# Gate/up groups in fours with shared remainders, one PSUM tag, and x transposed by DMA, in a fused state-space and gated-unit kernel

## The chip, the core and the metric

One core of one Trainium2 chip. The metric is the device time of one execution in microseconds (us), the median of several. The profile's span runs from the first to the last instruction and is about 1.8 us shorter than the time. TensorE is PE below, its weight loads PEld, VectorE DVE, ScalarE ACT, SyncE SP; SPq and ACTq are their instruction streams issuing DMAs. PSUM is the memory in which matmuls add up their results; a slot is the piece of it that a group of matmuls holds until ACT has copied it out (its drain).

## The reference, cut to what matters

```python
xn = layernorm(x)                               # x: 1 x 2048 x 576, bf16
# A: diagonal complex state space, 576 states
Bu = einsum("bld,pd->blp", xn, B_bar)
h[t] = Lam_bar * h[t-1] + Bu[t]                 # 2048 steps
yA = 2 * real(einsum("blp,dp->bld", h, C)) + xn * Dskip
# B: gated unit, F = 4608
yB = (sigmoid(xn @ w_gate) * (xn @ w_up)) @ w_down
out = x + yA + yB
```

## The kernel before

The 2048 rows are four blocks (`nb`) of 512, handled two at a time; F is cut in three, so there are six stages of 24 gate/up groups and 8 down-projection steps. Contraction 576 is four times 128 and a remainder of 64 rows: the remainder matmuls of gate (upper 64 rows of the array) and up (lower 64) run side by side. A scheduler (`bg`) strews the LayerNorm of later blocks and the state-space work on DVE between the groups. A normalised tile is `xn`, its transpose `xT`; `brre` holds the remainder rows of B, `hst` the states, `acc` the running sum of a row tile. Cut:

```python
def ln_transpose(tt):                           # one of 16 row tiles
    ptr = psum.tile([P, NXK, P], BF16, name="ptr", tag="pg")
    for k in range(NXK):
        nc.tensor.transpose(ptr[:, k, :], xn[:, c0:c0 + P], ident[:])
    nc.scalar.copy(xT[nb][:, :, tl * P:(tl + 1) * P], ptr[:])
# ...
def gu_step(sb, c, f, nb):                      # one gate/up group
    pg = psum.tile([P, TB], FP32, name="pg", tag="pg")
    pu = psum.tile([P, TB], FP32, name="pu", tag="pu")
    rem_first = (nb % 2 == 0)
    if rem_first: rem()                         # two 64-row matmuls
    for (ps, gi) in ((pg, 0), (pu, 1)):
        for k in range(KF):
            nc.tensor.matmul(ps[:], w[:, gi, k, fs], xt_[:, k, :], ...)
    if not rem_first: rem()
    nc.scalar.activation(sT[:], pg[:], ACT.Sigmoid)
    nc.scalar.copy(uT[:], pu[:])
    nc.vector.tensor_mul(h[:], sT[:], uT[:])
# ... start: blocks 0 and 1 are normalised and transposed whole, with
# their residuals, before the first group; later: queue_ln per tile:
#     ln_stats, ln_rstd (square root on ACT), ln_norm, ln_transpose, ln_resid
# ... second stage: load_ct (four C transposes by DMA), then
def pack_bt():
    nc.sync.dma_start(brre[0:H, :], brre[H:P, :])
```

Of the kernel before, what the change touches and what calls it, by code (L numbers as in the profile page):

```python
# [19 lines left out]
ROW_TILED = True  # L20


class Background:



    def __init__(self):
        self.queue = deque()
        self.credit = 0.0

    def add(self, cost, fn):
        self.queue.append((cost, fn))

    def step(self, us):
        self.credit = min(self.credit + us, 4.0)
        while self.queue and self.queue[0][0] <= self.credit:
            cost, fn = self.queue.popleft()
            self.credit -= cost
            fn()

    def drain(self):
        while self.queue:
            self.queue.popleft()[1]()
# [3 lines left out]
def kernel(  # L47
# [19 lines left out]
    H = 64  # L67
# [7 lines left out]
    TB = 512  # L75
    NB_SB = 2
    NSB = S // (TB * NB_SB)
# [3 lines left out]
    PT = NS // P  # L81
    FC = 12
    NC = F // P // FC
    DH = D // 2
    XW = R0 + 2 * H if ROW_TILED else R0 + 3 * H
    NXK = KF + 1 if ROW_TILED else KF + 2
    T_G = 1.95 if ROW_TILED else 2.16
# [9 lines left out]
    evp = ctx.enter_context(tc.tile_pool(name="evp", bufs=3))  # L97
    ssmp = ctx.enter_context(tc.tile_pool(name="ssmp", bufs=1))
    psum = ctx.enter_context(tc.tile_pool(name="psum", bufs=2, space=bass.MemoryType.PSUM))


    def load_x(tt, eng):
        xt = lnp.tile([P, D], BF16, name="xt", bufs=6)
        eng.dma_start(xt[:], x[tt * P:(tt + 1) * P, :])
        return xt
# [4 lines left out]
    def load_wgu(key, pair, eng):  # L110
        f0 = pair * 2 * P
        w = wpool.tile([P, 2, KF, 2 * P], BF16, name="wgu", bufs=3)
        wr = wpool.tile([P, 2 * P], BF16, name="wrem", bufs=3)
        fs = slice(f0, f0 + 2 * P)
        eng.dma_start(w[:, 0], B_w_gate[0:R0, fs].rearrange("(k p) f -> p k f", p=P))
        eng.dma_start(wr[0:H, :], B_w_gate[R0:D, fs])
        eng.dma_start(w[:, 1], B_w_up[0:R0, fs].rearrange("(k p) f -> p k f", p=P))
        eng.dma_start(wr[H:P, :], B_w_up[R0:D, fs])
        wgu_t[key] = (w, wr)
# [7 lines left out]
    xts = {}  # L127
    for tt in range(TT_B):
        xts[tt] = load_x(tt, nc.sync)
    load_wgu((0, 0), 0, nc.scalar)  # L130

    ident = consts.tile([P, P], BF16, name="ident")
    make_identity(nc, ident[:])
# [4 lines left out]
    XN_BUFS = 3  # L138
    xn_bufs = []
    for i in range(XN_BUFS):  # L140
        xn_i = consts.tile([P, XW], BF16, name=f"xn{i}")
        if not ROW_TILED:
            nc.vector.memset(xn_i[:, D:D + H], 0.0)
        xn_bufs.append(xn_i)

    for tt in range(TT_B, 2 * TT_B):
        if tt < 6:
            xts[tt] = load_x(tt, nc.sync)
    load_wgu((0, 1), 1, nc.sync)
    dskip_rows = consts.tile([P, D], BF16, name="dskip_rows")  # L150
    nc.gpsimd.dma_start(dskip_rows[:], A_Dskip.partition_broadcast(P))


    BN = nc.vector.BN_STATS_DIM
    mvs = {}
    accs = {}
# [3 lines left out]
    def ln_stats(tt):  # L160
        xt = xts[tt]
        st = lnp.tile([P, 2, BN], FP32, name="bnst", bufs=2)
        for gi in range(2):
            nc.vector.bn_stats(st[:, gi, :], xt[:, gi * DH:(gi + 1) * DH])  # L164
        mv = lnp.tile([P, nc.vector.BN_AGGR_DIM], FP32, name="mv", bufs=10)
        nc.vector.bn_aggr(mv[:], st[:])
        mvs[tt] = mv

    rstds = {}

    def ln_rstd(tt):
        r = lnp.tile([P, 1], FP32, name="rstd", bufs=10)
        nc.scalar.activation(r[:], mvs[tt][:, 1:2], ACT.Sqrt, bias=eps_t[:], scale=1.0)
        rstds[tt] = r

    xns = {}

    def ln_norm(tt):
        xn = xn_bufs[ln_count[0] % XN_BUFS]
        ln_count[0] += 1  # L180
        r = rstds[tt]
        nc.vector.reciprocal(r[:], r[:])
        nc.vector.tensor_scalar(xn[:, 0:D], xts[tt][:], mvs[tt][:, 0:1], r[:], ALU.subtract, ALU.mult)  # L183
        nc.vector.tensor_copy(xn[:, XW - H:XW], xn[:, R0:D])
        xns[tt] = xn

    def ln_transpose(tt):
        nb, tl = divmod(tt, TT_B)
        if tl == 0:
            xT[nb] = hpool.tile([P, NXK, TB], BF16, name="xT", bufs=3)  # L190
        xn = xns[tt]
        ptr = psum.tile([P, NXK, P], BF16, name="ptr", tag="pg")
        for k in range(NXK):
            c0 = k * P if k <= KF else R0 + H
            nc.tensor.transpose(ptr[:, k, :], xn[:, c0:c0 + P], ident[:])  # L195
        nc.scalar.copy(xT[nb][:, :, tl * P:(tl + 1) * P], ptr[:])  # L196

    def ln_resid(tt):
        tmp = lnp.tile([P, D], BF16, name="tmpxd", bufs=1)
        nc.vector.tensor_mul(tmp[:], xns[tt][:, 0:D], dskip_rows[:])  # L200
        acc = accp.tile([P, D], FP32, name="acc", bufs=16)
        nc.vector.tensor_add(acc[:], xts[tt][:], tmp[:])  # L202
        accs[tt] = acc


    for tt in range(TT_B):
        ln_stats(tt)
        ln_rstd(tt)
        if tt >= 1:
            ln_norm(tt - 1)  # L210
            ln_transpose(tt - 1)
        if tt >= 2:
            ln_resid(tt - 2)
    ln_norm(TT_B - 1)
    ln_transpose(TT_B - 1)
    ln_resid(TT_B - 2)
    ln_resid(TT_B - 1)
    for tt in range(6, 2 * TT_B):
        xts[tt] = load_x(tt, nc.sync)
    for tt in range(TT_B, 2 * TT_B):  # L220
        ln_stats(tt)
        ln_rstd(tt)
        ln_norm(tt)
        ln_transpose(tt)
        ln_resid(tt)
    for pr in range(2, 3):
        load_wgu((0, pr), pr, nc.sync)
    load_wd((0, 0), 0, nc.sync)


    NU = PT + 1
# [9 lines left out]

    def load_bt():
        W0 = D - P
        nc.sync.dma_start_transpose(btre[:], A_B_re[:, 0:R0])
        nc.sync.dma_start_transpose(brre[:], A_B_re[:, W0:D])
        nc.sync.dma_start_transpose(btim[:], A_B_im[:, 0:R0])
        nc.sync.dma_start_transpose(brim[:], A_B_im[:, W0:D])

    def load_ct():
        W0 = NS - P  # L250
        nc.sync.dma_start_transpose(ctre[:], A_C_re[:, 0:R0])
        nc.sync.dma_start_transpose(ctim[:], A_C_im[:, 0:R0])
        nc.sync.dma_start_transpose(ctp[:], A_C_im[:, W0:NS])
        nc.sync.dma_start_transpose(ctw[:], A_C_re[:, W0:NS])
        nc.sync.dma_start(ctp[0:H, :], ctw[H:P, :])

    def pack_bt():
        if ROW_TILED:
            nc.sync.dma_start(brre[0:H, :], brre[H:P, :])
# [4 lines left out]
        if not ROW_TILED:  # L264
            nc.gpsimd.memset(btp[0:H, KF, :], 0.0)


    lre = consts.tile([P, NU], FP32, name="lre")
    lim = consts.tile([P, NU], FP32, name="lim")
    ldt = consts.tile([P, NU], FP32, name="ldt")  # L270
    for (dst, src) in ((lre, A_Lambda_re), (lim, A_Lambda_im), (ldt, A_log_dt)):
        for pt in range(PT):
            nc.gpsimd.dma_start(dst[:, pt:pt + 1], src[pt * P:(pt + 1) * P].rearrange("(a b) -> a b", b=1))
        for h0 in (0, H):
            nc.gpsimd.dma_start(dst[h0:h0 + H, PT:NU], src[R0:NS].rearrange("(a b) -> a b", b=1))
    sg_pm = consts.tile([P, 1], FP32, name="sg_pm")
    nc.gpsimd.memset(sg_pm[0:H, :], 1.0)
    nc.gpsimd.memset(sg_pm[H:P, :], -1.0)
    iota = consts.tile([P, TB], FP32, name="iota")
    nc.gpsimd.iota(iota[:], pattern=[[1, TB]], base=0, channel_multiplier=0,  # L280
                   allow_small_or_imprecise_dtypes=True)

    r5 = consts.tile([P, NU], FP32, name="r5")
    thc = consts.tile([P, NU], FP32, name="thc")
    qre = consts.tile([P, NU], FP32, name="qre")
    qim = consts.tile([P, NU], FP32, name="qim")
    nqre = consts.tile([P, NU], FP32, name="nqre")
    c512 = consts.tile([P, NU], FP32, name="c512")
    s512 = consts.tile([P, NU], FP32, name="s512")
# [8 lines left out]
    def sincos(u, sin_out, cos_out):  # L298
        a = small("sc_a")
        b = small("sc_b")  # L300
        for (dst, add) in ((sin_out, 0.0), (cos_out, 0.25)):
            nc.vector.tensor_scalar_add(a[:], u[:], add)
            nc.vector.tensor_scalar_add(b[:], a[:], MAGIC)
            nc.vector.scalar_tensor_tensor(b[:], b[:], MAGIC, a[:], ALU.subtract, ALU.subtract)
            nc.scalar.activation(dst[:], b[:], ACT.Sin, bias=zero_t[:], scale=SIN_SCALE)

    def per_state():
        dt = small("dt")
        nc.scalar.activation(dt[:], ldt[:], ACT.Exp)
        nc.vector.tensor_mul(r5[:], dt[:], lre[:])  # L310
        nc.scalar.activation(r5[:], r5[:], ACT.Exp)
        nc.vector.tensor_mul(thc[:], dt[:], lim[:])
        nc.vector.tensor_scalar_mul(thc[:], thc[:], 1.0 / TWO_PI)
        sn, cs = small("sn"), small("cs")
        sincos(thc, sn, cs)
        u = small("u512")
# [364 lines left out]
```

## Time and profile before

| | before |
|---|---|
| time, median | 620.75 us |
| span | 618.7 us |
| PE busy | 543.7 us (88%) |
| granted PE clock, mean | 0.956 |
| PE waiting for the norms (DVE) | 50.9 us |
| PE waiting for the remainder rows of B (`brre`) | 10.2 us |

Read it from PE: an idle microsecond there is on the chain that ends last, and an idle microsecond of DVE or ACT is not. In a wait row the columns are: who waited, `<-` for whom, us in total, times, longest.

### The profile page before, as it was taken

The numbers are of one execution on the slowest core, as the hardware profiler recorded it, in microseconds if no ns is written. First come the engines' busy times: TensorE is split into PE (matmuls) and PEld (weight loads), VectorE is DVE, ScalarE is ACT, GpSimd is POOL, SyncE is SP. The second block draws the span as 40 slices with busy tenths as digits, with TensorE's granted clock in tenths as the row PEclk, the third lists the DMA queues.
The fourth block names the chain that finished last, engine by engine and source line by source line (L and its number), as shares of the span: only waits on it lengthen the run. The fifth ranks groups of instructions, "written<-read, shape, count | busy, mean of one in ns | idle before, by whom it ended". The sixth has DMA issues, their size and how long they took to land.

```text
span 618.7 us, 8129 instructions
## 1 busy us (share of the span) xinstructions
PE 543.7 (88%) x3140; PEld 282.2 (46%) x3140; DVE 327.8 (53%) x738; ACT 229.8 (37%) x395; POOL 13.0 (2%) x34
## 2 busy tenths in 40 slices
PE   1399979957999997666889999999999999999967
PEld 1133357422357432223664333763335763336745
DVE  6711259772576573322244665674656665555451
ACT  3355543533530465551014555115553025552000
POOL 7000000000000000000000000000000000000000
PEclk9999999997999997777899999999999999999979
DMA  7227520262230142113000423202423012400000
GB/s 164 56 58 173 153 58 0 59 146 72 69 108 1 39 122 66 56 45 101 18 17 2 114 80 95 58 0 59 116 77 95 1 40 63 145 4 11 30 11 29
DMA packets 72405, 40.34 MB, mean 65 GB/s; under 512 B 17424, under 2 KB 72336, under 8 KB 72368
## 3 DMA queue, kind: packets, MB, share of 16 engines
q1 hardware_dynamic: 68896, 39.09, 22.8%
q0 software_dynamic: 2256, 0.16, 0.6%
q10 hardware_dynamic: 1216, 0.59, 0.3%
q8 instruction: 24, 0.39, 0.3%
q14 instruction: 13, 0.11, 0.1%
HBM read 34.36 MB, written 2.36 MB: 59 GB/s over the span
## 4 chain that ended last, share of the span: by engine, by line
PE 80%; DVE 11%; ACT 4%; DMA 2%; SPq 2%; issue 1%; ACTq 0%; DVEq 0%
PE pd L546 26%; PE pg L524 21%; PE pu L524 20%; PE pg L518 6%; PE pa L385 2%; PE pb L385 2%; DVE bnst L164 1%; DVE xn L183 1%; PE ptr L195 1%; PE pa L389 1%; DVE acc L202 1%; ACT L535 1%; ACT uT L536 1%; DVE rnd L346 1%; DVE acc L567 1%
## 5 line engine op out<-in xcount | busy, mean ns | idle before, releaser
L524 PEld LDWEIGHTS <-wgu 128*128 128x128 bf16 x1152 | 109.0, 100 | 157.1 <-issue 45.7
L538 DVE TENSOR_TENSOR hT<-sT,uT 128x512 bf16<-128x512 bf16 x144 | 60.5, 422 | 186.8 <-ACT uT L536 186.7
L546 PE MATMUL pd<-wd,hT 128*128 128x288 bf16 x1152 | 151.5, 294 | 4.8 <-DVE acc L567 4.8
L524 PE MATMUL pg<-xT,wgu 128*128 128x512 bf16 x576 | 155.6, 394 | 0.0
L524 PE MATMUL pu<-xT,wgu 128*128 128x512 bf16 x576 | 152.7, 389 | 0.0
L535 ACT ACTIVATE sT<-pg 128x512 bf16<-128x512 f32 x144 | 86.0, 597 | 127.3 <-PE pu L519 101.1
L546 PEld LDWEIGHTS <-hT 128*128 128x128 bf16 x1152 | 114.6, 100 | 39.3 <-issue 8.0
L536 ACT CAST uT<-pu 128x512 bf16<-128x512 f32 x144 | 83.9, 582 | 24.2 <-PE pu L524 24.2
L195 PE MATMUL ptr<-ident,xn 128*128 128x128 bf16 x80 | 10.6, 292 | 50.9 <-DVE xn L183 50.9
L519 PE MATMUL pu<-xT,wrem 64*128 64x512 bf16 x144 | 47.4, 393 | 0.0
L518 PE MATMUL pg<-xT,wrem 64*128 64x512 bf16 x144 | 47.4, 393 | 0.0
L567 DVE TENSOR_TENSOR acc<-acc,pd 128x576 f32<-128x576 f32 x36 | 26.9, 751 | 26.5 <-PE pd L546 26.5
L564 DVE TENSOR_TENSOR ob<-acc,pd 128x576 bf16<-128x576 f32 x16 | 12.0, 753 | 53.8 <-PE pd L546 53.8
L546 PEld LDWEIGHTS <-hst 128*128 128x128 bf16 x288 | 27.9, 98 | 13.5 <-DVE hst L467 5.3
L393 ACT COPY bure<-pa 128x512 f32<-128x512 f32 x16 | 9.4, 585 | 62.9 <-PE pb L390 62.9
L195 PEld LDWEIGHTS <-xn 128*128 128x128 bf16 x80 | 6.8, 127 | 55.5 <-DVE xn L183 55.5
L546 PE MATMUL pd<-ctim,hst 128*128 128x288 bf16 x128 | 26.2, 286 | 0.7 <-DVE hst L473 0.7
L546 PE MATMUL pd<-ctre,hst 128*128 128x288 bf16 x128 | 26.2, 286 | 0.3 <-DVE hst L467 0.3
L437 DVE TENSOR_TENSOR_SCAN gre<-r,g0re,wre 128x512 bf16<-128x512 f32 x20 | 25.5, 1277 | 0.0
L518 PEld LDWEIGHTS <-wrem 64*128 64x128 bf16 x144 | 9.1, 94 | 32.7 <-issue 32.6
L405 ACT COPY bure<-pa 128x512 f32<-128x512 f32 x4 | 2.3, 585 | 52.9 <-PE pa L400 36.3
L196 ACT COPY xT<-ptr 128x640 bf16<-128x640 bf16 x16 | 11.1, 692 | 25.9 <-PE ptr L195 25.9
(118 smaller groups left out, 375.2 us busy)
## 6 DMA issues: line engine op xcount, KB each, us to landing
wd<-in_B_w_down_dram SPq DMA_DIRECT2D x36, 288.0 KB, 3.6
wgu<-in_B_w_gate_dram SPq DMA_DIRECT2D x35, 256.0 KB, 2.9
wgu<-in_B_w_up_dram SPq DMA_DIRECT2D x35, 256.0 KB, 3.6
xt<-in_A_x_dram SPq DMA_DIRECT2D x16, 144.0 KB, 3.4
out_dram<-ob SPq DMA_DIRECT2D x16, 144.0 KB, 1.8
wrem<-in_B_w_gate_dram SPq DMA_DIRECT2D x35, 32.0 KB, 2.6
wrem<-in_B_w_up_dram SPq DMA_DIRECT2D x35, 32.0 KB, 3.2
wgu<-in_B_w_gate_dram ACTq DMA_DIRECT2D x1, 256.0 KB, 3.4
```

Of the source, the lines that this page charges most:

```text
L195: nc.tensor.transpose(ptr[:, k, :], xn[:, c0:c0 + P], ident[:])
L385: nc.tensor.matmul(ps[:], bt[:, k, cols], xt_[:, k, :], start=(k == 0), stop=False)
L437: nc.vector.tensor_tensor_scan(gre[:], r_bc, tmps["wre"][:], g0re[:, col], ALU.mult, ALU.add)
L518: nc.tensor.matmul(pg[:], wr[0:H, fs], xt_[0:H, KF, :], start=rem_first, stop=not rem_first)
L519: nc.tensor.matmul(pu[:], wr[H:P, fs], xt_[H:P, KF, :], start=rem_first, stop=not rem_first)
L524: nc.tensor.matmul(ps[:], w[:, gi, k, fs], xt_[:, k, :], start=(k == 0 and not rem_first), stop=(k == KF - 1 and rem_first))
L535: nc.scalar.activation(sT[:], pg[:], ACT.Sigmoid)
L536: nc.scalar.copy(uT[:], pu[:])
L538: nc.vector.tensor_mul(h[:], sT[:], uT[:])
L546: nc.tensor.matmul(pd[:, a, 0:DH], lhsT, rhs[:, a * DH:(a + 1) * DH], start=first, stop=last)
L564: nc.vector.tensor_add(halves(ob[:]), halves(acc[:]), pd[:, :, 0:DH])
L567: nc.vector.tensor_add(halves(acc[:]), halves(acc[:]), pd[:, :, 0:DH])
```

## The change

Intent: keep PE's stream free of waits and of switches between 64-row and 128-row matmuls. Core of the diff; the rest is scheduling and renaming.

```diff
-    psum = ... bufs=2                      # tags pg, pu and pd
+    psum = ... bufs=PE_SLOTS               # 4 slots of two banks, one tag "ps"
+    def emit_cluster(groups):              # four gate/up or state-input groups
+        first, second = groups[:n1], groups[n1:]
+        for g in first:  g.open(); g.full(True, False)
+        for g in second: g.open()
+        for g in first:  g.rem(False, True)
+        for g in second: g.rem(True, False)
+        for g in first:  g.evac()
+        for g in second: g.full(False, True); g.evac()
-    ln_transpose (PE) for every tile
+    def ln_dma_transpose(tt):              # blocks 1, 2 and 3
+        nc.sync.dma_start_transpose(xT_tile(nb)[:, :, tl*P:(tl+1)*P], xns[tt][:])
+    # block 0: PE transposes, and the first two groups take it tile by tile
+    # as 128-column matmuls, after 8 matmuls on a zero tile
+    for tt in range(TT_B + 1):
+        if tt < TT_B: ln_stats(tt); ln_std(0, tt, tt + 1)
+        if tt >= 1: ln_recip(...); ln_norm(tt - 1); start_transpose(tt - 1)
+        if tt >= 2: start_mms(tt - 2)
+    exp_first()                            # the state space's exponentials
+    # then in the background: residuals 0, 1; loads of x tiles 6, 7;
+    # statistics of block 1; one square root for four tiles; norms, transposes
+    bt_loads = [...]                       # B transposes and pack_bt, one a cluster, stage 1
     load_wgu: bufs=3 -> 4;  wd: one pair beyond those done, as before, but two pairs now end together
+    last output step in two halves, each added and sent by itself
```

## The prediction

> **What bounds the kernel now.** I read the page first (its head and slices), then the waits of TensorE alone, then TensorE's timeline around the longest waits, and last the timelines of VectorE at the start and of the Sync queue.
>
> ```profile
> span 618.7 us, 8129 instructions
> PE 543.7 (88%) x3140; PEld 282.2 (46%) x3140; DVE 327.8 (53%) x738; ACT 229.8 (37%) x395; POOL 13.0 (2%) x34
> ...
> PE   1399979957999997666889999999999999999967
> ...
> PEclk9999999997999997777899999999999999999979
> ```
>
> PE is the longest engine and the chain that ended last is 80% PE. The dips (the first slice, slice 9, slices 16 to 19, the last) are where it waits, and the clock falls in most of the same slices. Idle PE is 618.7 - 543.7 = 75.0 us. The waits name nearly all of it:
>
> ```profile
> engine line waited for: us in total, times, longest us
> PE ptr L195 <- DVE xn L183: 50.9, 16, 7.0
> PE pa L389 <- DMA brre<-brre: 10.2, 1, 10.2
> PE pd L546 <- DVE acc L567: 4.8, 3, 3.5
> PE pd L546 <- DVE hst L467: 4.7, 2, 4.4
> ```
>
> 50.9 + 10.2 + 4.8 + 5.4 (with a 0.7 us row for another hst line) = 71.3, and PE's tail after its last matmul is 3.6: 74.9. Of the 50.9, 23.4 lie in the first 29 us, 27.5 in the middle, where blocks 2 and 3 are normalised between matmuls. One such place:
>
> ```profile
> 233.31 1.03 PE L524 MATMUL pu<-xT,wgu 128*128 128x512 bf16 x4
> 234.27 0.39 PE L518 MATMUL pg<-xT,wrem 64*128 64x512 bf16 x1
> 234.27 0.39 PE L519 MATMUL pu<-xT,wrem 64*128 64x512 bf16 x1
> 238.49 0.72 PE L195 MATMUL ptr<-ident,xn 128*128 128x128 bf16 x5 [3.83 <-DVE xn L183]
> 239.14 0.60 PE L518 MATMUL pg<-xT,wrem 64*128 64x512 bf16 x1
> 239.14 0.61 PE L519 MATMUL pu<-xT,wrem 64*128 64x512 bf16 x1
> 239.68 1.89 PE L524 MATMUL pg<-xT,wgu 128*128 128x512 bf16 x4
> ```
>
> The transpose stands in PE's in-order stream and waits 3.83 us. Afterwards four matmuls take 1.89 us instead of 1.03. In starts, the pitch of a 512-column matmul is 427 ns instead of 216. Counting such matmuls after every gap gives some 20 us of slow running on top of the 75: 2.0 at the start, 2.7 after the brre wait, 1.7 in the first down-projection, 11.3 in the middle, 2.7 near the end. The third cost is in steady state:
>
> ```profile
> 208.40 0.39 PE L518 MATMUL pg<-xT,wrem 64*128 64x512 bf16 x1
> 208.40 0.39 PE L519 MATMUL pu<-xT,wrem 64*128 64x512 bf16 x1
> 208.62 0.38 PE L518 MATMUL pg<-xT,wrem 64*128 64x512 bf16 x1
> 208.63 0.38 PE L519 MATMUL pu<-xT,wrem 64*128 64x512 bf16 x1
> 208.94 0.82 PE L524 MATMUL pg<-xT,wgu 128*128 128x512 bf16 x3
> ```
>
> Remainder pairs run side by side and follow each other at 0.22 us, but the step from 64 to 128 rows takes 308 ns instead of 217, and the step into it 312 instead of 216: 0.187 us for both. I count 198 such steps, 99 pairs, 18.5 us.
>
> **What the Trainium skill says.** "TensorE: Matmul & The Clock Gate", Part 1: the array runs at half clock until it was busy for about 3.4 us and falls back after an idle window as long; the 427 and 216 ns agree, and so do the slow stretches after gaps of 3.8 to 5.5 us. "TensorEngine Tiling (Array Packing)", Key Properties: changing the tiling mode drains the array; the 0.187 us agrees. "ScalarE: Activation LUTs", What ACT_TABLE_LOAD costs: about 1283 ns for every switch of set; the trace has 1283 ns each time, and normalisation (square root) between sigmoids pays it twice. "DMA: Bandwidth & Descriptors", DMA Transpose (X-bar): transposes go out from Sync or ScalarE only and stand beside ordinary DMAs; here 128-column transposes of A_B hold the Sync queue 1.25 us each and land after 3.1 to 4.4.
>
> **The change part by part.**
> 1. Steady work. 1296 matmuls of 512 columns x 0.2163 = 280.3; 164 remainder pairs or singles x 0.220 = 36.1; 1440 of 288 columns x 0.1226 = 176.5; 80 transposes 8.8; 18.5 of row switches: 520.2. After: the same matmuls. A cluster of four groups pays one pair of switches: 164 groups (144 gate/up, 20 state-input) with part clusters and single catch-ups make about 49 clusters, 9.2 us: 9.3 saved. One PSUM tag of four two-bank slots is the whole PSUM; in steady state a slot is reopened 4 us or more after its group's stop, and one group's drain is 0.60 + 0.58 on ACT, so PE should not wait; ACT needs 4.7 us in a cluster of 8.
> 2. Start. Before, the first gate/up matmul is at 29.06 and two groups are done at about 34.9. After, only block 0's four tiles are on this path, without the residual (0.45 + 0.76 us a tile). VectorE per tile is 1.03 + 0.16 + 0.43 + 0.18 = 1.8 us from about 6.3 (DMA 3.0, square-root table 1.28, as before), so the last norm ends near 11.7. PE per tile is 5 transposes (0.6) plus 16 matmuls of 128 columns, 0.107 each cold: 2.3 us, so PE is the later one: 7.2 to about 16, remainders near 17. Saved 34.9 - 17 = 17.9, cold part included.
> 3. Middle. Blocks 2 and 3 leave PE's stream: 27.5 + 11.3 cold = 38.8, and 8 transposes of 0.53 = 4.2 (block 1's are in part 2).
> 4. brre. B transposes are issued one per cluster and packed in the first stage, long before use; C's come later: 10.2 + 2.7 = 12.9.
> 5. Angles move under the gate/up groups, and PSUM for the down-projection is four deep: 4.8 + 1.7 = 6.5.
> 6. The state chain: VectorE per unit 9.4 us, 20 units 166; my sum of the budget that the new scheduler hands out per stage ends the chain in the fifth stage, so the last stage doesn't wait: 5.4 + 2.7 = 8.1. The split last output saves 0.4.
> Removed: 9.3 + 17.9 + 38.8 + 4.2 + 12.9 + 6.5 + 8.1 + 0.4 = 98.1.
> 7. Added: block 1 comes due after only eight groups of block 0, at 17 + 12.5 = 29.5. Its chain: VectorE is blocked by the first exponential (behind ACT's copy of tile 3 and a table load) until about 16.5; two residuals 2.4, two statistics 2.1, two products 0.9, two more statistics 2.1: 24; ACT's square root between two table loads, then the third group's sigmoid and copy and product: 27.3; reciprocal and four norms of 0.6: 30; four transposes at some 1.3 us each on the Sync queue, the last one landing 3 later: 33 to 35. PE waits about 5 and then runs cold for a while: 7.5 in all. The late sigmoid also delays a PSUM slot, inside the same wait.
> 8. Added, small: down-projection weights are now fetched one pair ahead instead of two, state-input groups as clusters of one in down-projection stages: 3.
> Net 98.1 - 10.5 = 87.6: 620.7 - 87.6 = 533. From the other side: PE resumes on block 1 at 34.5, 498 us of steady work less eight groups (12.5) remain, 2 cold, 3 small, 3.2 tail: 530.7 span, and the times stand about 2 above the span: 532.6. I take 532.
>
> **The rivals.**
> A. Block 1 is ready in time, or its wait is 2 us: 524 to 527. For it: the transposes may overlap in the queue, and warm matmuls at the start may leave the clock up. Against it: VectorE's in-order queue as counted in 7.
> B. VectorE becomes the bound. Its 328 us would be 62% of 530, and in stages 2 and 3 products (0.42) plus background (1.37) fill 1.8 of each 2.0 us. If the scheduler's costs are below the real ones (an angle is booked 1.35, its three instructions here take 0.48 + 0.43 + 0.69 = 1.6), VectorE falls behind, output buffers of ACT fill, PE waits: 545 to 560. For most pieces the booked costs are at or above the trace's (1.85 against 1.79), so I give it little.
> C. The Sync queue. Transposes, weight fetches and loads that wait for VectorE share one in-order queue; a weight pair held back behind a transposition wait costs PE 2 to 4 us and a cold restart, once a stage: 540 to 550. Four buffers instead of three speak against it.
> D. All waits were hidden anyway: excluded, since PE's idle time here is on the chain that ends last.
>
> **Range and chances.** The sure part (parts 1, 3, 4) is 65 us. The start and block 1 are uncertain by 5 either way, B and C by 10 upward, A by 7 downward: 521 to 546. Faster by over 2% is anything under 608; all the additions would have to be eight times as large to lose it: 0.98.
>
> **What would show it.** Step 1: about half as many 64/128 switches, still 308 to 312 ns. Step 2: first full-width gate/up group near 17 us. Steps 3 and 4: no PE wait on xn after the first 20 us and none on brre; clock at full in the middle slices. Steps 5 and 6: no PE wait on acc or hst over 1 us. Step 7: a PE wait near 30 us whose releaser is the DMA of xT. Step 8: none over 1 us at the stage borders. It would be wrong if PE shows new waits on ACT's drains (PSUM slots) or on weight DMAs, or if the pitch in clusters is not 216 ns.

## The result, and the profile after

The changed kernel takes 526.53 us (525.29 to 526.59, 4 runs), before 620.75 (620.28 to 621.76, 4 runs). The ratio is 0.8476, 95% interval 0.8459 to 0.8492. A ratio here and below is the mean time of one kernel's fast runs over that of the other's of the same rounds, so not quite the ratio of the medians.

The page's head, and its slices of PE and of the granted clock:

```profile
span 524.7 us, 7898 instructions
PE 508.6 (97%) x3096; PEld 283.5 (54%) x3136; DVE 319.3 (61%) x716; ACT 200.2 (38%) x367; POOL 9.3 (2%) x25
...
PE   7879999999999999999999999999999999999997
...
PEclk9989999999999999999999999999999999999999
```

Only the first three slices and the last one have holes. PE's waits:

```profile
PE pgu L463 <- DMA xT<-xn: 3.8, 1, 3.8
PE pgu L463 <- ACT uT L475: 1.6, 1, 1.6
...
PE pd L557 <- DVE ob L565: 0.5, 1, 0.5
```

No wait is left on `brre`, `acc` or `hst`; on xn 1.5 us, at the start. The first two rows are both of the start: the wait for block 1, and a PSUM slot held by a late drain. PE's timeline there (start, duration, instruction, count, and in brackets the idle time before it and its releaser), and the Sync queue's line for the four transposes:

```profile
27.83 1.67 PE L463 MATMUL pgu<-xT,wgu 128*128 128x512 bf16 x7 [0.16 <-issue]
33.26 5.08 PE L463 MATMUL pgu<-xT,wgu 128*128 128x512 bf16 x15 [3.75 <-DMA xT<-xn]
```

```profile
26.45 5.29 SPq L232 DMA_TRANSPOSE xT<-xn  x4
```

PE finishes block 0's eight groups at 29.5 and waits until block 1 has been normalised and four transposes of 1.3 us each have gone out one behind the other. Then fifteen matmuls take 5.08 us, where fifteen take 3.40 elsewhere: eight starts in a row stand some 427 ns apart, as after the wait in the prediction.

In steady state a cluster looks like this (a state-input group, `pbu`, and three gate/up groups):

```profile
101.93 0.39 PE L503 MATMUL pbu<-xT,brre 64*128 64x512 bf16 x1
101.93 0.39 PE L503 MATMUL pbu<-xT,brim 64*128 64x512 bf16 x1
102.15 0.81 PE L468 MATMUL pgu<-xT,wrem 64*128 64x512 bf16 x6
102.90 3.63 PE L463 MATMUL pgu<-xT,wgu 128*128 128x512 bf16 x16
```

All four groups' remainders follow one another and there is one return to 128 rows. The traces have 198 changes between 64 and 128 rows before and 96 after. The first down-projection, before and after:

```profile
79.85 6.05 PE L546 MATMUL pd<-wd,hT 128*128 128x288 bf16 x48
89.39 7.71 PE L546 MATMUL pd<-wd,hT 128*128 128x288 bf16 x48 [3.48 <-DVE acc L567]
```

```profile
66.88 23.68 PE L557 MATMUL pd<-wd,hT 128*128 128x288 bf16 x192
```

Before, it ran from 79.85 to 110.40 with three waits for `acc`; after, all 192 matmuls stand in one piece. (Some PE records are missing from the traces, so PE's busy time after is a little too low; the gaps above are not of that kind.)

### The profile page after: what moved, and what is told of

Same layout as the page of the kernel before. It is cut to its first block, busy times and chain, and to the rows that moved or that the text cites. A ratio compares the mean times of both kernels' runs of the same rounds, so it can differ in the third digit from the quotient of the medians.

```text
span 524.7 us, 7898 instructions
## 1 busy us (share of the span) xinstructions
PE 508.6 (97%) x3096; PEld 283.5 (54%) x3136; DVE 319.3 (61%) x716; ACT 200.2 (38%) x367; POOL 9.3 (2%) x25
## 4 chain that ended last, share of the span: by engine, by line
PE 94%; DVE 3%; DMA 1%; issue 1%; ACT 1%; ACTq 0%
PE pgu L463 46%; PE pd L557 34%; PE pgu L468 6%; PE pbu L498 6%; PE pbu L503 1%; DVE bnst L206 1%; DMA xt<-in_A_x_dram 1%; DMA xT<-xn 1%; DVE acc L238 0%; PE ptr L718 0%; DVE xn L220 0%; DVE hT L477 0%; DVE tmpxd L236 0%; ACT L474 0%; ACT L299 0%
## 5 line engine op out<-in xcount | busy, mean ns | idle before, releaser
L463 PE MATMUL pgu<-xT,wgu 128*128 128x512 bf16 (+1 forms) x1170 | 259.6, 375 | 7.8 <-DMA xT<-xn 3.8
L474 ACT ACTIVATE sT<-pgu 128x512 bf16<-128x512 f32 x144 | 86.9, 604 | 142.3 <-PE pgu L468 106.1
L475 ACT CAST uT<-pgu 128x512 bf16<-128x512 f32 x144 | 84.7, 588 | 0.0
L576 DVE TENSOR_TENSOR acc<-acc,pd 128x576 f32<-128x576 f32 x32 | 24.1, 752 | 30.3 <-PE pd L557 30.3
L468 PE MATMUL pgu<-xT,wrem 64*128 64x512 bf16 x288 | 38.7, 378 | 0.0
L407 DVE TENSOR_TENSOR_SCAN gre<-r,g0re,wrim 128x512 bf16<-128x512 f32 x20 | 25.6, 1278 | 0.0
L414 DVE TENSOR_TENSOR_SCAN gim<-r,g0im,wrim 128x512 bf16<-128x512 f32 x16 | 20.4, 1274 | 0.0
L498 PE MATMUL pbu<-xT,btim 128*128 128x512 bf16 x62 | 16.3, 379 | 0.1
L498 PE MATMUL pbu<-xT,btre 128*128 128x512 bf16 x57 | 16.1, 379 | 0.4
L393 DVE TENSOR_TENSOR wrim<-T,bure 128x512 bf16<-128x512 bf16 x20 | 13.7, 685 | 0.0
L394 DVE TENSOR_TENSOR tq<-T,buim 128x512 bf16<-128x512 bf16 x20 | 13.7, 685 | 0.0
```

What stands on the lines that cost most here:

```text
L393: nc.vector.tensor_mul(w, t1, a[:])
L407: nc.vector.tensor_tensor_scan(gre[:], r_bc, w[:, 0, :], g0re[:, col], ALU.mult, ALU.add)
L414: nc.vector.tensor_tensor_scan(gim[:], r_bc, w[:, 1, :], g0im[:, col], ALU.mult, ALU.add)
L463: nc.tensor.matmul(self.ps[:, gi, cols], self.w[:, gi, k, self.fs], xT[self.nb][:, k, cols], start=start and k == 0, stop=stop and k == KF ...
L468: nc.tensor.matmul(self.ps[:, gi, :], self.wr[rows, self.fs], xT[self.nb][rows, KF, :], start=start, stop=stop)
L474: nc.scalar.activation(sT[:], self.ps[:, 0, :], ACT.Sigmoid)
```

## Experiments

Twelve runs, eleven variants and the changed kernel again, all with the right result, in three batches of four, each on one chip. "Before" was 621.2, 621.8 and 621.5 us in the three batches, and the changed kernel run again in the third batch took 526.54.

**1. Before, with blocks 2 and 3 transposed by DMA alone.**

```diff
     def ln_transpose(tt):
+        if nb >= 2:
+            nc.sync.dma_start_transpose(xT[nb][:, :, tl*P:(tl+1)*P], xn[:])
+            return
```

> The kernel before with one part of the change alone: the tiles of blocks 2 and 3 are transposed by DMA instead of by TensorE. My theory (TensorE pays for waiting in its own stream, plus slow matmuls afterwards): 27.5 us of waits, 11.3 us of slow matmuls and 4.2 us of transposes go, so about 578 us (573 to 588), and the middle slices show the full clock. Rival (the wait only moves: the normalisation chain on VectorE is what is late, and the next reader of the transposed block waits instead): 600 us or more, with a new TensorE wait on the transposed block.

Measured 579.52 us (ratio 0.9328, 0.9299 to 0.9356), 41.7 us less. The stretch from 233 to 292 us, before and in this run; the columns are the stretch, its length, busy us with instruction counts of PE, PEld, DVE, ACT and POOL, clock, DMA share and GB/s:

```profile
233.00:292.00 59.00, 40.20 (x171) 16.45 (x168) 17.16 (x46) 27.91 (x40) 0.00 (x0) 0.77 0.21 58
```

```profile
233.00:292.00 59.00, 57.00 (x379) 35.19 (x382) 32.38 (x85) 26.23 (x41) 0.00 (x0) 1.00 0.40 96
```

In these 59 us PE is busy 57.00 us instead of 40.20 and the clock is 1.00 instead of 0.77. (The counts are no measure of the work: 264 of the 379 are the shorter 288-column matmuls, before 42 of the 171.) PE's wait for the norms falls to 23.9 us, which is the start, and its wait for the DMA's xT is 0.2 us; new are 1.4 us of waits on ACT. The rival, that the wait only moves to the next reader, falls.

**2. Before, with the copy of B's remainder rows right behind B's transposes.**

```diff
     def load_bt():
         ...
+        nc.sync.dma_start(brre[0:H, :], brre[H:P, :])
     def pack_bt():
-        nc.sync.dma_start(brre[0:H, :], brre[H:P, :])
```

> The kernel before with one line moved: the copy of the B remainder rows goes out right behind the B transposes in the first stage instead of behind the C transposes in the second. My theory: the 10.2 us wait and about 2.7 us of slow matmuls go: 608 us (606 to 611). Rival (the state-input group would then wait for something else that is late as well, or the Sync queue holds back weights in the first stage): 614 us or more, with a new wait of TensorE.

Measured 607.07 us (ratio 0.9775, 0.9748 to 0.9802): 14.1 us less, clear of noise, and no row for `brre` among PE's waits. In the chain that ended last, before, the copy stands behind C's transposes, and PE had been waiting since 132.9:

```profile
129.84 3.16 SPq L251
...
137.38 3.04 DMA ctw<-in_A_C_re_dram
141.05 2.04 DMA brre<-brre
```

One transfer queued behind unrelated ones had cost that much.

**3 and 4. The changed kernel with more row switches: each group's remainders behind its own full matmuls; and groups in twos.**

```diff
         for g in first:
             g.open(); g.full(True, False)
+            g.rem(False, True)
-        for g in first: g.rem(False, True)
-        for g in second: g.rem(True, False)
+        # second: rem of its first group, drains of first, then
+        # full / rem / full for the second's groups
```

```diff
-            while groups and len(quad) < 4:
+            while groups and len(quad) < 2:
```

> The changed kernel, clusters of four kept, but inside a cluster each group's remainders follow its own full matmuls, so about 78 more pairs of switches between 64 and 128 rows; the PSUM use, the drains and the order of groups stay. My theory (a pair of switches costs 0.187 us of TensorE's time): +14.6 us, 541 us (538 to 544). Rival (the clusters help because the drains of ACT have more time, the switches themselves are hidden): within 2 us of 526.5.

> The changed kernel with groups in twos instead of fours. My theory: about 38 more pairs of switches, +7 us: 533.5 us (531 to 537), nothing else, because in steady state a PSUM slot is free long before it is reopened. Rival (fours are needed for PSUM or for the drains): over 540 us with TensorE waiting on ACT.

Measured 541.45 us (ratio 0.8712, 0.8682 to 0.8742) and 533.80 (0.8594, 0.8569 to 0.8619). The traces have 246 and 172 changes against 96: 75 and 38 pairs more, for 14.9 and 7.3 us, so 0.199 and 0.191 us a pair, where the step lengths of the trace had given 0.187. (Each difference is good to about 1 us, so the second price is the rougher one.) Neither run shows a wait that the changed kernel has not. The drains and slots of the first are those of the changed kernel, so the switch itself is what costs; and fours aren't needed for PSUM's sake.

**5. The changed kernel with blocks 2 and 3 transposed on PE again.**

```diff
-            bg.add(0.0, lambda tt=tt: ln_dma_transpose(tt), urgent=True)
+            bg.add(0.0, lambda tt=tt: ln_pe_transpose(tt), urgent=True)
+            bg.gap(True)
```

> The changed kernel with the DMA transposes of blocks 2 and 3 undone: TensorE transposes them into a PSUM slot, one tile a background step, the statistics still taken in one batch per block. My theory (what costs is that TensorE's in-order stream waits for VectorE at the point where the transpose stands): 8 transposes of 0.53 us and waits of 1 to 2 us each, little slow running because the waits are shorter than the 3.8 to 5.5 us of before: +12 to +20 us, 540 us. Rival (the gain of the middle came from batching the statistics, which takes the square root out of the wait, and not from the DMA): under +6 us.

Measured 550.65 us (ratio 0.8865, 0.8822 to 0.8908): 24.1 us more, above what I expected. Its PE timeline around the first two tiles of block 2:

```profile
191.82 1.90 PE L471 MATMUL pgu<-xT,wgu 128*128 128x512 bf16 x8
198.39 0.71 PE L239 MATMUL ptr<-ident,xn 128*128 128x128 bf16 x5 [4.68 <-DVE xn L220]
198.90 3.62 PE L471 MATMUL pgu<-xT,wgu 128*128 128x512 bf16 x8
204.54 0.71 PE L239 MATMUL ptr<-ident,xn 128*128 128x128 bf16 x5 [2.03 <-DVE xn L220]
```

The waits before the eight transposes sum to 15.6 us: block 2's are 4.68, 2.03, 1.21 and 2.56, block 3's 1.2 to 1.4, and only the last four and one more are the 1 to 2 that I expected. Eight matmuls behind the first take 3.62 instead of 1.90. So slow running comes back, after the first wait, which isn't shorter than those before, and also after the waits of 1.21 and 2.56, which have only 0.44 us of transposes between them: the trace's clock record stands at half for 10.2 us around the first and for 3.4 us after these. I had thought that shorter waits would spare it. With the statistics batched and the square root out of the way, the transposes' place in PE's stream still costs 24 us (15.6 of waits, 4.2 of transposes, the rest slow running), so the rival falls.

**6. The changed kernel with the first exponentials later.**

```diff
     start_mms(TT_B - 1)
-    exp_first()
...
+    bg.add(0.4, exp_first); bg.gap()
     bg.add(1.5, angles_small)
```

> The changed kernel with the first exponentials moved from the start to just ahead of the small angles, so VectorE doesn't stand 4.5 us behind ACT before it begins block 1. My theory (block 1 is late because its VectorE chain starts late): the 3.8 us wait for the transposed block and its 1.9 us of slow matmuls and the 1.6 us wait on a PSUM slot mostly go: 520 to 523 us. Rival (the transposes' time in the Sync queue, 5.3 us for four, or the load of the last x tiles sets it): 525 us or more, the wait stays.

Measured 525.53 us (ratio 0.8455, 0.8419 to 0.8492); the changed kernel has 0.8475 in its own second run, so no clear difference. DVE's line, then PE's:

```profile
13.98 0.46 DVE L236 TENSOR_TENSOR tmpxd<-xn,dskip_rows 128x576 bf16<-128x576 bf16 x1 [3.08 <-DMA dskip_rows<-in_A_Dskip_dram]
```

```profile
31.86 6.53 PE L463 MATMUL pgu<-xT,wgu 128*128 128x512 bf16 x16 [3.72 <-DMA xT<-xn]
```

My theory fell in this form. DVE, no longer held by ACT, stood for the skip weights, which the change had moved behind the state's small loads. PE went on with block 1 at 31.86 instead of 33.26, but after the same wait, since block 0's groups also ended sooner (the PSUM-slot wait was gone), and all of the next 16 matmuls ran slow (6.53 us, where the changed kernel's 16 took 5.30): 1.4 us earlier, given back by a longer slow stretch. Its length isn't shown to be the edit's doing: runs 3 and 4, which start as the changed kernel does, also have a slow stretch of 6.8 us behind a wait of 3.7, the changed kernel one of 3.4. What an earlier block 1 is worth stays open here.

**7. The changed kernel with block 0 taken whole.**

```diff
-        if tt >= 2:
-            start_mms(tt - 2)
-    start_mms(TT_B - 1)
+    for g in start_groups:
+        g.full(False, False)
```

> The changed kernel with block 0 taken whole: the first two groups' matmuls come after all four tiles are transposed, as 512-column matmuls. My theory: the last tile's copy lands at 13.9 us as now; two groups take 3.5 us at full clock, or up to 6.8 if TensorE runs slow after its near-idle start, where now the last tile's part takes 0.9: +3 to +6 us, part of it given back because block 1's chain does not move and the wait near 30 us shrinks by as much: net +0 to +3 us. Rival (tile by tile is worth its full 3 to 6 us on the end): +4 us or more.

Measured 526.30 us (ratio 0.8472, 0.8437 to 0.8507), no difference. The wait for block 1 is 2.2 us instead of 3.8 and the slot wait is gone: as expected, most of what tile by tile saves at the start is given back there. But PE goes on with block 1 at 34.52 instead of 33.26, so not all of it; the rest comes from the clock, which I hadn't expected: no slow matmuls follow the shorter wait, and the next 16 take 3.61 us instead of 5.30.

**8 and 9. The changed kernel with each gate/up product computed twice, and three times.**

```diff
             nc.vector.tensor_mul(h[:], sT[:], uT[:])
+            nc.vector.tensor_mul(h[:], sT[:], uT[:])      # a second one more for run 9
```

> The changed kernel with the product of each gate/up group computed twice on VectorE (0.42 us x 144 = 60 us more work, same result). My theory (VectorE is not the bound, but in the second and third stage it is filled to 1.8 of each 2.0 us): it falls behind there by about 0.2 us a group and catches up under the down-projections: +1 to +8 us. Rival (VectorE has become the bound): +30 us or more. If TensorE alone counted: no change.

> The changed kernel with every gate/up product computed three times on VectorE (121 us more than the changed kernel). Doubling cost nothing: VectorE then was busy 59 of 62 us in the fullest stage. Here about 355 us of VectorE work stand in the 352 us of the first four stages, so it has to fall behind: +4 to +20 us, 530 to 546, with TensorE waiting on VectorE or ACT. If it costs nothing again, VectorE's order leaves more room than I can account for.

Measured 526.16 us (ratio 0.8466, 0.8432 to 0.8501) and 555.11 (0.8932, 0.8907 to 0.8956). Both expectations missed: twice costs nothing, three times costs 28.6 us and not 4 to 20. The stretch from 110 to 172 us in the changed kernel, and with the product taken twice and three times:

```profile
110.00:172.00 62.00, 61.42 (x359) 32.40 (x366) 50.11 (x110) 25.97 (x49) 0.00 (x0) 1.00 0.39 102
```

```profile
110.00:172.00 62.00, 61.42 (x356) 32.50 (x362) 59.37 (x134) 25.33 (x49) 0.00 (x0) 1.00 0.38 101
```

```profile
110.00:172.00 62.00, 53.51 (x257) 22.94 (x262) 59.35 (x137) 26.95 (x52) 0.00 (x0) 0.94 0.37 98
```

DVE is busy 50.1 of these 62 us in the changed kernel and about full at 59.4; the second product used that room up, and PE lost nothing. With the third, DVE falls behind, ACT waits for its buffers, and PE waits on ACT up to 6.0 us at a time with slow matmuls after the longest waits. So VectorE isn't the bound, but in this stretch it has only some 12 of 62 us left before it is. I had underrated both its room and, once it is late, the price: PE's waits come with slow restarts.

**10 and 11. Block 1's whole chain ahead of the rest, with block 0 tile by tile and whole.**

```diff
-    xt ... bufs=6
+    xt ... bufs=8                          # tiles 6, 7 loaded at once
-    exp_first()
+    for tt in range(4, 8): ln_stats(tt)
+    ln_std(1, 0, TT_B)
+    ...                                    # remainders of the first two groups
+    ln_recip; norms and DMA transposes of tiles 4 to 7 (residuals 0, 1 between)
+    bg: residuals 2 to 7, exp_first, gap, angles
-    evp bufs=4
+    evp bufs=3
```

> Moving the exponentials alone only moved VectorE's block from ACT to the load of the skip weights, and the last two x tiles came late behind residuals and weights. So here the whole chain of block 1 goes first: eight x buffers, so the last two tiles are loaded at once; its four statistics, square root (no table switch), norms and DMA transposes come straight after block 0's, ahead of the residuals (but two, for the xn buffers); the exponentials later; drain buffers three instead of four to make room. My theory (the wait near 30 us is VectorE's order, not the DMA): the four transposes are issued from about 16 us on and have landed by 24, TensorE reaches block 1 near 28 without a wait, a slow stretch or a wait on a PSUM slot: 3.8 + 1.9 + 1.6 less, 519.5 us (518 to 521.5). Rival (something else of the start comes due, weights or the first drains): 523 us or more.

> The same, but with block 0 taken whole again. My theory: tile by tile was worth nothing in the changed kernel because the wait for block 1 set the time at which work goes on; with that wait gone it is worth what it saves at the start, 2 to 5 us: 522 to 525 us. Rival (tile by tile is worth nothing anyway): within 1 us of the run before.

Measured 528.56 us (ratio 0.8510, 0.8487 to 0.8533) and 528.14 (0.8506, 0.8485 to 0.8526): 2 us slower than the changed kernel, where I expected 7 us faster. Run 10 on ACT and on PE:

```profile
27.80 0.21 ACT L303 ACTIVATE r<-r 128x5 f32<-128x5 f32 x1 [8.09 <-DVE r L302]
```

```profile
30.43 3.57 PE L465 MATMUL pgu<-xT,wgu 128*128 128x512 bf16 x8 [7.87 <-ACT uT L477]
```

PE doesn't wait for block 1's xT any more. But I had put the exponentials behind six residuals in DVE's order; ACT, in order too, stood 8.09 us for a product of 128x5 elements between its two exponentials and drained nothing, so a PSUM slot came free late and PE stood 7.87. The tail of the chain had only changed its owner. (Three drain buffers instead of four went with the edit; no run separates them.) Run 11 has the same fault (3.5 us) and thus says nothing on what tile by tile is worth without the wait. Whether a start without any wait gives the 5 to 7 us stays open: no further kernel was run, and none here beat the changed one clearly.

## Why the prediction was right

The range was 521 to 546 and the time 526.5; 532 was 5.5 too high.

- **Step 1, switches.** Predicted 9.3 us for 50 pairs fewer. There are 51 fewer; at 0.195 us, the mean of runs 3 and 4, that is 9.9.
- **Steps 2 and 7, start and block 1.** Predicted 17.9 - 7.5 = 10.4 together. The first stage's 24 groups now end at 66.88 instead of 79.85: 13.0, of which about 1 belongs to the switches. The first full-width group starts at 15.5 instead of "near 17": I took all tile matmuls at 107 ns, but the last 32 took 2.00 us, 62 each. PE went on with block 1 at 33.3, in the predicted window of 33 to 35. The wait was 3.8 and not "about 5", with 1.7 of slow matmuls (8 x 0.211), and the slot wait 1.6, which came on its own, at 23.6, and not inside that wait.
- **Step 3, the middle.** Predicted 43.0; run 1, this part alone, gave 41.7.
- **Step 4, brre.** Predicted 12.9; run 2 gave 14.1.
- **Step 5, first down-projection.** Predicted 6.5; the stage takes 23.5 us (192 matmuls) instead of 30.5: 7.0.
- **Step 6, end of the state chain.** Predicted 8.1; the last write of `hst` begins at 390 us, among the fifth stage's groups, and the waits of 5.4 us with their slow matmuls are gone. This is read from the traces, no run has it alone. The split output step was wrong in sign: PE waits 0.5 us for DVE to read the first half before it may write the second, and the step from one to the other takes 0.83 us in all, 0.7 more than without; the tail after the last matmul is 3.4 instead of 3.6.
- **Step 8, small additions.** Predicted 3; the trace shows no wait at the stage borders. Its one row on a weight DMA, 0.2 at the start, reads as a missing record: the same gap stands at eight other places with no releaser. The reason given was misread, too: both kernels ask for down-projection weights one pair beyond the pairs done. What changed is that two pairs end together, so in the first five stages the last weights are asked for 1.7 to 3.7 us before the down-projection starts, where it was 6.2 or more. They land up to 1.6 us after its start and are needed at its 21st matmul, 2.45 us in: late, but still in time. This is the term most mis-sized.

Parts summed: 41.7 + 14.1 + 8.8 (switches outside the first stage) + 13.0 + 7.0 + 8.1 - 0.5 = 92.2 of the 94.2 us measured. (The 41.7, 14.1 and 8.8 rest on runs, the others on the traces alone.) The parts add up because each one takes idle or slow time out of one engine's stream, and all that comes after it moves forward.

The prediction's second sum has a slip: its terms give 528.2 for the span, not 530.7, so 530 for the time. Against 524.7 measured, 3.5 less, 1.2 is the earlier start of block 1 and most of the rest is step 8, less what the split output costs. Rival A (524 to 527) came near the time, but not by its way: block 1 was not in time. Rivals B and C did not happen; runs 8 and 9 show how near B was.

## What to carry to other kernels

Where one engine sets the end, list what stands in its in-order stream and waits for others, and price each as wait plus slow restart; such prices, unlike shares of busy time, could be added up here to within 2 us. Move the waiting instruction to a queue that can wait (here the transposes, worth 42 us), and mode switches to places where several share one. When a wait near the start is to be removed, follow the order of every in-order engine behind it: twice here the wait went to the next engine in line, once to a load and once to a tiny exponential.

## What the Trainium skill lacked or had wrong

- "TensorEngine Tiling (Array Packing)", Key Properties, says that a change of tiling mode drains the array but gives no cost: 0.187 us a pair of changes in the trace, 0.191 and 0.199 by the two runs that add pairs.
- "DMA: Bandwidth & Descriptors", DMA Transpose (X-bar), gives no time that such a transpose holds its queue; Latency and other measured facts has rates only, 261 GB/s in one kernel with a non-contiguous middle dimension and some 350 to 400 for the contiguous case. Here four transposes of 128 x 640 bf16 (164 KB each) from SBUF to SBUF held the Sync queue 5.29 us, 1.3 us each or 124 GB/s, and PE could go on 1.5 us after that.
- "TensorE: Matmul & The Clock Gate", Part 1, has a free-running window of 3413 ns and no rule for how long the clock stays down after a given wait. The traces agree with such a window: by their clock records the slow stretches between matmuls last 3.41, 6.83 or 10.24 us, one, two or three such windows. After the slot wait of 1.6 us in the changed kernel none followed, after 3.75 us one of 3.41 (eight slow matmuls), in run 6 after 3.72 us one of 6.83 (fourteen recorded ones). One window more or less at half clock is, by estimate, 1.7 us of the kernel's time. Eight matmuls on zeros at 1.3 to 4.9 us did not keep the clock up: in the changed kernel the 128-column matmuls of the first two tiles still came at 106 ns, and at 56 only from 13 us on; in its second run and in runs 3, 4, 7 and 10 the clock was up for one window from 4.0 to 5.5 us on and then fell again.
- "ScalarE: Activation LUTs", What ACT_TABLE_LOAD costs, adds some 1380 ns of drain to the 1283 ns of each switch, 2.66 us in all. Where ACT had work queued (at 235.06 before, at 13.93 after), the traces have 1.31 us from the end of the instruction before the load to the start of the one after it, so no such drain; the prediction, which left the drain out, was nearer.
